# Low parts of every second first-layer weight tile subtracted by GpSimd instead of VectorE

## The chip, the cores and the metric

The kernel runs on one core of a Trainium2 chip. The metric is the device time of one execution in microseconds, the median of several runs. The engines of a core work side by side, each through its own queue in order: TensorE (PE; its weight loads are shown as PEld), VectorE (DVE), ScalarE (ACT), GpSimd (POOL) and SyncE (SP), which issues all the DMAs here.

## What is computed

A windowed attention with 32 global tokens (4 batches, 8 heads, 512 local tokens each), and behind it two feed-forward layers over 2304 tokens, 512 wide with 2048 hidden units. The weights come in as 64-bit floats.

```python
def _moe_ref(x, w_in, w_out):          # first layer
    h = x @ w_in
    relu6 = np.clip(h + 3.0, 0.0, 6.0)
    g = h * relu6 / 6.0
    return (g @ w_out).astype(np.float32)

def _moe2_ref(x, w_in, w_out):         # second layer
    h = x @ w_in
    g = np.where(h > 0.0, h, np.exp(np.minimum(h, 0.0)) - 1.0)
    return (g @ w_out).astype(np.float32)
```

## The kernel before

Every product of the feed-forward layers is made from split operands: a number is kept as a high part, rounded to the format of the fast matrix product (fp32r), and a low part, which is the number minus its high part; three products (high by high, high by low, low by high) replace one. The first layer's weights are split into 16 tiles, one for each 128 hidden units. A tile `f` holds 128 x 512 numbers of `w_in` and 128 x 512 of `w_out`, so 1024 columns, and it is prepared in four steps by the class `Split`:

- `first` (line 126, ScalarE): converts the upper halves of the 64-bit words to a float in the buffer `f`.
- `second` (line 130, VectorE): a shift of that buffer.
- `third` (lines 134 and 137, VectorE): two merges of bits, each reading the raw words and the buffer, both in SBUF, and writing the buffer. The second needs the first's result.
- `fourth` (line 147, ScalarE, and 148, VectorE): the cast to the high part, then buffer minus high part, which gives the low part. Both operands of this subtraction lie in SBUF.

The buffer `f` has three places that the tiles use in turn (`f % 3`), so `first` of tile `k` waits until the subtraction of tile `k - 3` has read its buffer. Tile 0 is prepared in two halves, the others whole.

All this happens during the first 130 us, in between other work: the attention of the first tokens, and the first token chunk's passes through the layer. For a hidden tile `f` the pass is `up` (12 products on TensorE into `h`; the third one is the first that needs the low part of the weights), `act` (an activation of `h` on ScalarE, L600; a min-and-multiply on VectorE, L601, which reads `g` in SBUF and `h` in PSUM; a cast on ScalarE, L606; and a subtraction on VectorE, L608, which reads `g` and `gh` in SBUF and makes `gl`), and `down` (12 products into `acc`, the second of which needs `gl`). The attention's row minimum on VectorE (L390) reads one operand in PSUM and one in SBUF.

The order of all of it up to 130 us is written out by hand in a string, `SCHED`, read from left to right, and each step issues its instructions at that point. A letter is a step and a number its tile: `a`, `b`, `c`, `d` are the four steps of `Split`, `U` is `up`, `R` the activation and L601 and L606, `L` is L608, `D` is `down`; other letters load or belong to the attention. So the queue of every engine follows this string. After it a loop runs the other token chunks, and the second layer's weights are prepared beside them (`prepare`), starting with two loads (L160) into the buffers `f0` and `f2`, the first of which waits for the last subtraction of tile 15.

GpSimd has little to do: it makes the identity matrix at the start and, after 420 us, two subtractions of 128x768 (L668).

Of the kernel before, what the change touches and what calls it, by code (L numbers as in the profile page):

```python
# [10 lines left out]
F32 = mybir.dt.float32  # L11
# [57 lines left out]
def tile_kernel(ctx, tc, qkW, vW, qkG, vN, vG, masks, w1, w2, out):  # L69
    nc = tc.nc  # L70
# [41 lines left out]
    class Split:  # L112
# [28 lines left out]
        def fourth(self, s=slice(2)):  # L141
            if s.start in (None, 0):
                wslot[self.m, self.f] = pool.tile(
                    [P, 2, 2, DM], F32R, name=f"w{self.m}_{self.f}", tag="w", bufs=NF
                )
            hi, lo = wslot[self.m, self.f][:, 0], wslot[self.m, self.f][:, 1]
            nc.scalar.copy(hi[:, s], self.wf[:, s])
            nc.vector.tensor_sub(lo[:, s], self.wf[:, s], hi[:, s].bitcast(F32))  # L148

    splits = [Split(0, f) for f in range(NF)]  # L150
    wd = [dr.tile([P, 12 * DM], F32, name=f"wd{p}", tag=f"wd{p}") for p in range(NF // 2)]
# [183 lines left out]
    class Local:  # L335
# [111 lines left out]
        def stages(self, nxt=None):  # L447
            def first():
                self.scores()
                for r in range(2):  # L450
                    self.softmax(r)
                if nxt is not None:
                    nxt.load_qk()

            def second():
                for r in range(2):
                    self.transposed(r)

            def third():
                self.values()  # L460
                self.normalised()
                if nxt is not None:
                    nxt.load_v()

            def fourth():
                self.turned()
                self.split()

            loads = ((1.9, 1.8), (0, 1.2), (1.2, 0), (0.7, 0.6))
            if self.n < CHUNKS[0] + CHUNKS[1]:  # L470
                loads = ((1.9, 1.8), (0, 1.2), (0.4, 1.8), (0.7, 0.6))
            return list(zip((first, second, third, fourth), loads))
# [198 lines left out]
    class Super:  # L671
# [139 lines left out]
        def up(self, g, k):  # L811
# [11 lines left out]
            if k == 1:  # L823
                self.s1 = self.staged(g, "s1", "gh")
                nc.scalar.copy(self.s1, self.a)
            elif k == 2:
                self.c11 = self.staged(g, "c11", "gl")
                nc.vector.tensor_add(self.c11, self.b, self.s1)  # L828
                self.after(1, lambda c=self.c11: self.act(g, 0, c))
            elif k == 6:  # L830
                self.s2 = self.staged(g, "s2", "gh")
                nc.scalar.copy(self.s2, self.a)
            elif k == 5:
                s4, c22 = self.staged(g, "s4", "gh"), self.staged(g, "c22", "gl")
                nc.scalar.copy(s4, self.a)  # L835

                def fourth(b=self.b):
                    nc.vector.tensor_add(c22, b, s4)
                    self.after(1, lambda: self.act(g, 3, c22))

                self.after(1, fourth)
            elif k == 3:
                self.act(g, 1, self.a)
            elif k == 4:
                c21 = self.staged(g, "c21", "gl")
                nc.vector.tensor_add(c21, self.b, self.s2)
                self.after(2, lambda: self.act(g, 2, c21))
# [243 lines left out]
```

## Time and profile before

| | |
|---|---|
| median of 3 runs | 864.99 us (864.95 to 866.28) |
| the profiled execution, its own time | 864.55 us |
| its span, first to last instruction | 862.8 us |
| TensorE busy | 841.0 us, 97% |
| VectorE busy | 516.3 us, 60% |
| ScalarE busy | 429.5 us, 50% |
| GpSimd busy | 4.4 us, 1%, 8 instructions |
| mean granted TensorE clock | 0.997 |

Busy time is the sum of the instructions' durations on an engine; it is an average over stages that differ. The stage of the first 130 us is read apart in the rows below. A start of an instruction is given in us from the span's beginning; its row may name in brackets how long the engine sat idle before it, and what ended that.

### The profile page before, as it was taken

How to read it: one execution, taken by the hardware profiler on the slowest of the kernel's cores; microseconds unless marked ns; L12 is line 12 of the kernel's file. 1: busy time of each engine (PE TensorE's matmuls, PEld its weight loads, DVE VectorE, ACT ScalarE, POOL GpSimd, SP SyncE). 2: the span in 40 equal slices, each digit the busy share in tenths (PEclk: the TensorE clock that was granted, in tenths of full speed). 3: DMA queues.
4: the chain of work that ended last, by engine and by line, in shares of the span. 5: the costliest groups of instructions: out<-in, count | busy, mean ns of one | idle time of the engine just before them, and what ended most of it. 6: DMA issues, size and time to landing. Idle time of an engine off the chain costs nothing.

```text
span 862.8 us, 15804 instructions
## 1 busy us (share of the span) xinstructions
PE 841.0 (97%) x6424; PEld 727.1 (84%) x6424; DVE 516.3 (60%) x1125; ACT 429.5 (50%) x835; POOL 4.4 (1%) x8
## 2 busy tenths in 40 slices
PE   8899999999999999998999999999999999999997
PEld 7677778898988899887888889998998888888886
DVE  5788984666565556664655557444456665445443
ACT  6577655454544455543433346454445664444441
POOL 0000000000000000000000000000000000000000
PEclk9999999999999999999999999999999999999999
DMA  9958213656674765563589783946852656444102
GB/s 370 418 210 327 84 52 108 229 180 196 235 258 136 236 230 201 196 201 117 190 296 330 271 315 142 385 172 265 344 187 84 258 208 255 147 147 147 49 1 98
DMA packets 37657, 178.43 MB, mean 207 GB/s; under 512 B 4304, under 2 KB 6224, under 8 KB 25680
## 3 DMA queue, kind: packets, MB, share of 16 engines
q1 hardware_dynamic: 37584, 177.42, 56.9%
q8 instruction: 50, 0.82, 0.4%
q14 instruction: 23, 0.19, 0.1%
HBM read 143.33 MB, written 34.08 MB: 206 GB/s over the span
## 4 chain that ended last, share of the span: by engine, by line
PE 84%; DVE 7%; DMA 4%; ACT 3%; issue 2%; SPq 0%; ACTq 0%; DVEq 0%
PE acc L574 30%; PE h L574 22%; PE ua L574 9%; PE yt L574 9%; PE ub L574 7%; DMA v<-in_vW 1%; PE O L413 1%; PE S L381 1%; PE T L90 1%; DVE f L134 1%; DVE g L601 1%; DVE f L137 1%; DMA raw<-in_w 1%; DVE w L148 1%; DMA qk<-in_qkW 1%
## 5 line engine op out<-in xcount | busy, mean ns | idle before, releaser
L574 PE MATMUL acc<-gh,w 128*128 128x384 f32 (+1 forms) x640 | 199.5, 367 | 0.0
L574 PE MATMUL h<-x1h,w 128*128 128x384 f32 (+1 forms) x640 | 195.7, 367 | 1.6 <-DVE w L148 1.5
L574 PEld LDWEIGHTS h<-x1h,w 128*128 128x128 f32 x640 | 118.5, 189 | 20.1 <-issue 5.3
L574 PEld LDWEIGHTS acc<-gh,w 128*128 128x128 f32 x640 | 119.1, 189 | 13.4 <-issue 0.6
L574 PE MATMUL acc<-gl,w 128*128 128x384 f32 (+1 forms) x320 | 115.6, 361 | 0.8 <-DVE gl L608 0.8
L574 PE MATMUL h<-x1l,w 128*128 128x384 f32 (+1 forms) x320 | 115.5, 361 | 0.2 <-DVE x1l L445 0.2
L601 DVE SCALAR_TENSOR_TENSOR g<-g,h 128x384 f32<-128x384 f32 (+1 forms) x80 | 48.6, 607 | 110.4 <-ACT g L600 110.2
L600 ACT ACTIVATE g<-h,half 128x384 f32<-128x384 f32 (+1 forms) x80 | 49.8, 622 | 93.0 <-PE h L574 92.9
L606 ACT CAST gh<-g 128x384 fp32r<-128x384 f32 (+1 forms) x96 | 52.8, 550 | 77.0 <-DVE g L601 64.9
L574 PE MATMUL ua<-xs,ws 128*128 128x384 f32 (+1 forms) x384 | 88.0, 364 | 0.0
L574 PEld LDWEIGHTS ua<-xs,ws 128*128 128x128 f32 x384 | 70.4, 188 | 10.7 <-ACT s L835 0.3
L608 DVE TENSOR_TENSOR gl<-g,gh 128x384 fp32r<-128x384 f32 (+1 forms) x96 | 57.4, 599 | 24.6 <-ACT gh L606 24.1
L574 PEld LDWEIGHTS acc<-gl,w 128*128 128x128 f32 x320 | 60.4, 189 | 6.5 <-DVE gl L608 1.2
L574 PE MATMUL ub<-xs,ws 128*128 128x384 f32 (+1 forms) x288 | 65.7, 363 | 0.0
L574 PEld LDWEIGHTS h<-x1l,w 128*128 128x128 f32 x320 | 60.4, 189 | 6.1 <-DVE x1l L445 0.5
L574 PEld LDWEIGHTS ub<-xs,ws 128*128 128x128 f32 x288 | 52.7, 188 | 7.0
L877 DVE TENSOR_TENSOR y<-yt,y 128x512 f32<-128x512 f32 x49 | 33.8, 690 | 36.0 <-PE yt L574 35.5
L792 ACT ACTIVATE e<-c 128x384 f32<-128x384 f32 (+1 forms) x48 | 27.8, 580 | 45.8 <-DVE c L828 15.8
L574 PE MATMUL acc<-ws,gg_h 128*128 128x512 f32 x160 | 49.9, 393 | 0.0
L574 PE MATMUL yt<-ws,gg_h 128*128 128x512 f32 x160 | 49.9, 393 | 0.0
L795 DVE SCALAR_TENSOR_TENSOR e<-e,c 128x384 f32<-128x384 f32 (+1 forms) x48 | 30.0, 624 | 23.9 <-ACT e L793 23.3
L793 ACT ACTIVATE e<-e 128x384 f32<-128x384 f32 (+1 forms) x64 | 37.1, 579 | 2.0
(202 smaller groups left out, 1260.2 us busy)
## 6 DMA issues: line engine op xcount, KB each, us to landing
ws<-wd SPq DMA_DIRECT2D x48, 1024.0 KB, 5.4
raw<-in_w SPq DMA_DIRECT2D x16, 1024.0 KB, 11.7
raw<-in_w SPq DMA_DIRECT2D x32, 512.0 KB, 5.4
v<-in_vW SPq DMA_DIRECT2D x13, 1040.0 KB, 6.6
qk<-in_qkW SPq DMA_DIRECT2D x15, 704.0 KB, 6.0
qkG<-in_qkG SPq DMA_DIRECT2D x8, 608.0 KB, 4.6
wd<-ha SPq DMA_DIRECT2D x8, 512.0 KB, 4.8
wd<-hb SPq DMA_DIRECT2D x8, 512.0 KB, 4.8
```

What stands on the lines that cost most here:

```text
L90: nc.tensor.transpose(o, i, ident)
L134: nc.vector.scalar_tensor_tensor(w, self.high[:, s], -0x80000000, w, op0=ALU.bitwise_and, op1=ALU.bitwise_or)
L137: nc.vector.scalar_tensor_tensor(w, self.low[:, s], 29, w, op0=ALU.logical_shift_right, op1=ALU.bitwise_or)
L574: nc.tensor.matmul(o, a, b, start=first and i == 0, stop=last and i == len(pairs) - 1, skip_group_check=more)
L600: nc.scalar.activation(g, hp, AF.Relu, scale=1.0 / 6.0, bias=half)
L601: nc.vector.scalar_tensor_tensor(g, g, 1.0, hp, op0=ALU.min, op1=ALU.mult)
L606: nc.scalar.copy(gh, g)
L608: return lambda: nc.vector.tensor_sub(gl, g, gh.bitcast(F32))
L792: nc.scalar.activation(e, h, AF.Relu, scale=-1.0)
L793: nc.scalar.activation(e, e, AF.Exp, scale=-1.0)
L795: 1, lambda: nc.vector.scalar_tensor_tensor(e, e, -1.0, h, op0=ALU.add, op1=ALU.max)
L877: nc.vector.tensor_add(y, o, y)
```

## The change

The subtraction of `Split.fourth` is issued on GpSimd for tiles with an odd number (1, 3, ... 15) and stays on VectorE for even ones.

```diff
             hi, lo = wslot[self.m, self.f][:, 0], wslot[self.m, self.f][:, 1]
             nc.scalar.copy(hi[:, s], self.wf[:, s])
-            nc.vector.tensor_sub(lo[:, s], self.wf[:, s], hi[:, s].bitcast(F32))
+            sub = nc.gpsimd.tensor_sub if self.f % 2 else nc.vector.tensor_sub
+            sub(lo[:, s], self.wf[:, s], hi[:, s].bitcast(F32))
```

The line it adds shifts the numbers of all later lines by one, so L148 is L149 after, L601 is L602, and so on. Two places of the program show what it does to the queues. The first is VectorE's queue around tiles 5 and 6, before and then after; `f0_6` is the buffer of tile 6, `w0_5` the finished tile 5, `g0_0_3` the activation of hidden tile 3, and the brackets name the counters that an instruction waits for.

```order
L601 SCALAR_TENSOR_TENSOR g0_0_3_909<-g0_0_3_909,h0_0_3_840 128x512 [waits Activation_49]
L130 TENSOR_SCALAR f0_6_889<-f0_6_889 128x1024
L134 SCALAR_TENSOR_TENSOR f0_6_889<-raw0_6_697,f0_6_889 128x1024 [waits DMAHW4_49,DVE_49]
L137 SCALAR_TENSOR_TENSOR f0_6_889<-raw0_6_697,f0_6_889 128x1024 [waits DVE_49]
L148 TENSOR_TENSOR w0_5_931<-f0_5_836,w0_5_931 128x1024 [waits Activation_49]
L148 TENSOR_TENSOR w0_6_934<-f0_6_889,w0_6_934 128x1024 [waits Activation_49]
L608 TENSOR_TENSOR gl0_0_3_911<-g0_0_3_909,gh0_0_3_910 128x512
```

After it, the same stretch of VectorE's queue:

```order
L602 SCALAR_TENSOR_TENSOR g0_0_3_909<-g0_0_3_909,h0_0_3_840 128x512 [waits Activation_49]
L130 TENSOR_SCALAR f0_6_889<-f0_6_889 128x1024 [waits Pool_49]
L134 SCALAR_TENSOR_TENSOR f0_6_889<-raw0_6_697,f0_6_889 128x1024 [waits DMAHW4_49,DVE_49]
L137 SCALAR_TENSOR_TENSOR f0_6_889<-raw0_6_697,f0_6_889 128x1024 [waits DVE_49]
L149 TENSOR_TENSOR w0_6_934<-f0_6_889,w0_6_934 128x1024 [waits Activation_49]
L609 TENSOR_TENSOR gl0_0_3_911<-g0_0_3_909,gh0_0_3_910 128x512
```

The subtraction of tile 5 is gone from between the second merge of tile 6 and the subtraction of tile 6; nothing else changes place.

The second place is ScalarE's queue around tiles 7 to 9, before and then after; `f0_10` is the conversion (`first`) of tile 10 into the buffer that tile 7 used.

```order
L147 CAST w0_7_1160<-f0_7_891 128x1024
L126 ACTIVATE f0_10_1170<-raw0_10_1044 128x1024 [waits DMAHW4_49,DVE_49]
L147 CAST w0_8_1189<-f0_8_993 128x1024
L147 CAST w0_9_1192<-f0_9_1046 128x1024 [waits DMAHW5_49,DVE_49]
L600 ACTIVATE g0_0_7_1196<-h0_0_7_1176,half_65 128x512 [waits PE_49]
```

After it, the same stretch of ScalarE's queue:

```order
L147 CAST w0_7_1160<-f0_7_891 128x1024
L126 ACTIVATE f0_10_1170<-raw0_10_1044 128x1024 [waits DMAHW4_49,Pool_49]
L147 CAST w0_8_1189<-f0_8_993 128x1024
L147 CAST w0_9_1192<-f0_9_1046 128x1024 [waits DMAHW5_49,DVE_49]
L601 ACTIVATE g0_0_7_1196<-h0_0_7_1176,half_65 128x512 [waits PE_49]
```

The order is the same; the conversion of tile 10 now waits for GpSimd where it waited for VectorE, and the casts of tiles 8 and 9 still stand behind it. On GpSimd's queue the eight subtractions follow each other in the order of the tiles, each waiting for ScalarE's cast of its tile, ahead of the two of L668.

## Rows read from the trace of the kernel before

**Rows 1.** Windows: stretch, busy us and instructions by engine, clock, DMA share, GB/s.
```profile
35.00:60.00 25.00, 24.69 (x230) 18.89 (x229) 22.15 (x42) 19.54 (x36) 0.00 (x0) 1.00 0.79 318
60.00:90.00 30.00, 27.71 (x239) 20.93 (x238) 27.39 (x50) 18.63 (x37) 0.00 (x0) 1.00 0.58 236
90.00:130.00 40.00, 40.00 (x297) 31.95 (x296) 35.27 (x56) 23.88 (x43) 0.00 (x0) 1.00 0.22 76
```

**Rows 2.** Chain that ended last, two pieces: start, us, engine, output, line.
```profile
63.88 1.23 DVE f L137
...
87.01 2.60 PE h L574 x10
```

**Rows 3.** Waits of TensorE, 28 to 130 us: waiter, releaser, us, times, longest.
```profile
PE h L574 <- DVE w L148: 1.5, 2, 1.2
```

**Rows 4.** Groups by shape: operation, count, busy us and mean ns, idle before.
```profile
L668 POOL TENSOR_TENSOR x2l<-x2raw,x2h 128x768 fp32r<-128x768 f32 x2 | 3.7, 1845 | 436.5 <-ACT x2h L667 436.5
...
L148 DVE TENSOR_TENSOR w<-f,w 128x1024 fp32r<-128x1024 f32 x15 | 18.3, 1221 | 5.7 <-ACT w L147 5.7
...
L183 DVE TENSOR_TENSOR ob<-wo,ob 128x512 fp32r<-128x512 f32 x8 | 5.5, 689 | 1.6 <-ACT ob L179 1.6
```

**Rows 5.** Timeline, GpSimd and VectorE about 440 us: start, us, engine, operation, idle before.
```profile
439.64 1.85 POOL L668 TENSOR_TENSOR x2l<-x2raw,x2h 128x768 fp32r<-128x768 f32 x1 [14.86 <-ACT x2h L667]
...
440.11 1.92 DVE L183 TENSOR_TENSOR oa<-wo,oa 128x512 fp32r<-128x512 f32 x1 [0.56 <-ACT oa L179]
```

**Rows 6.** Timeline of VectorE about tiles 1 to 4.
```profile
36.63 1.22 DVE L148 TENSOR_TENSOR w<-f,w 128x1024 fp32r<-128x1024 f32 x1
37.76 1.22 DVE L134 SCALAR_TENSOR_TENSOR f<-raw,f 128x1024 int32<-128x1024 int32 x1
...
47.79 1.22 DVE L148 TENSOR_TENSOR w<-f,w 128x1024 fp32r<-128x1024 f32 x1
...
49.54 1.29 DVE L134 SCALAR_TENSOR_TENSOR f<-raw,f 128x1024 int32<-128x1024 int32 x1
```

**Rows 7.** Timelines of VectorE and of ScalarE about tiles 5 and 6.
```profile
65.03 2.41 DVE L148 TENSOR_TENSOR w<-f,w 128x1024 fp32r<-128x1024 f32 x2
67.36 0.69 DVE L608 TENSOR_TENSOR gl<-g,gh 128x512 fp32r<-128x512 f32 x1
...
62.54 1.05 ACT L147 CAST w<-f 128x1024 fp32r<-128x1024 f32 x1
65.14 1.05 ACT L147 CAST w<-f 128x1024 fp32r<-128x1024 f32 x1 [1.55 <-DVE f L137]
```

**Rows 8.** Timelines of VectorE and of ScalarE about tiles 7 to 10.
```profile
81.47 1.23 DVE L148 TENSOR_TENSOR w<-f,w 128x1024 fp32r<-128x1024 f32 x1 [2.33 <-ACT w L147]
...
84.59 1.23 DVE L137 SCALAR_TENSOR_TENSOR f<-raw,f 128x1024 int32<-128x1024 int32 x1
...
82.73 1.16 ACT L126 ACTIVATE f<-raw 128x1024 f32<-128x1024 f32 x1 [1.29 <-DVE w L148]
83.79 1.04 ACT L147 CAST w<-f 128x1024 fp32r<-128x1024 f32 x1
```

**Rows 9.** Timeline of TensorE: products that need `gl` (68.97) or a weight's low part.
```profile
68.97 0.39 PE L574 MATMUL acc<-gl,w 128*128 128x512 f32 x1
...
82.75 0.73 PE L574 MATMUL h<-x1h,w 128*128 128x512 f32 x2
...
87.01 0.73 PE L574 MATMUL h<-x1h,w 128*128 128x512 f32 x2 [1.19 <-DVE w L148]
```

**Rows 10.** TensorE's longest wait near 400 us, and the window (as rows 1) behind it.
```profile
399.87 0.84 PE L90 MATMUL XTG<-ident,xgg 128*128 128x128 f32 x4 [2.59 <-DVE xgg L554]
...
400.00:404.00 4.00, 4.00 (x16) 4.00 (x16) 1.84 (x5) 1.04 (x4) 0.00 (x0) 0.57 0.40 127
```

**Rows 11.** Second layer's first weight loads on SyncE's queue, and ScalarE's first use.
```profile
128.07 0.80 SPq L160 DMA_DIRECT2D raw<-in_w  x2
...
143.50 0.68 ACT L164 ACTIVATE wi<-raw 128x512 f32<-128x512 f32 x1
```

## The prediction

> **What bounds the kernel now.** I read the busy time by stretch first, then who waits for whom on TensorE, then the chain that ended last, then the queues around the eight moved subtractions. The busy shares say that TensorE is the bound of the whole: between 90 and 130 us it is busy 40.00 of 40 us [rows 1], and after that it waits only in a few places that the change doesn't touch. Whatever TensorE loses while the first layer's weights are being prepared is therefore lost at the end too, and whatever it gains there is gained. Between 35 and 90 us it is busy 24.69 of 25 and 27.71 of 30, so it idles 2.6 us there, and VectorE is almost as full: 22.15 of 25 and 27.39 of 30 [rows 1]. In that stretch the chain runs through VectorE: its second bit-merge (L137) at 63.88 is on it, and the chain returns to TensorE at 87.01 for good [rows 2]. TensorE's own waits on the moved line amount to 1.5 us in two places [rows 3]. So this is a stage with two full engines; a microsecond more on VectorE shows at the end, a microsecond less is worth 2.6 us altogether at most.
>
> **What the change takes away and adds.** Eight subtractions of 128x1024 (tiles 1, 3, ... 15) leave VectorE. One takes 1.22 us, and the next one starts 1.14 us after it, since ends overlap [rows 4, 6]. Half of them stand between 35 and 90 us: 4 x 1.14 = 4.6 us of VectorE's queue. GpSimd is idle there, and it has done the same operation in this trace, on 768 columns in 1.845 us [rows 4]. By columns, 1024 take 1.845 x 1024/768 = 2.46 us; if it scales as VectorE's does with part of it fixed, some 2.36. I take 2.46. No instruction or DMA is added, and TensorE's order is the same.
>
> **The price that decides: VectorE stands still meanwhile.** The trace has one place where VectorE's subtraction of two SBUF tiles met GpSimd's. GpSimd ran from 439.64 for 1.85 us, to 441.49. VectorE's 128x512 subtraction was begun at 440.11 and took 1.92 us, to 442.03 [rows 5], where the same one takes 0.69 us otherwise [rows 4]. It ended 0.54 us after GpSimd did, so it made no progress until GpSimd was through and then needed all but 0.15 us of its normal time. GpSimd took 1.85 us with and without that neighbour (the mean of the two is 1.845). I carry this over: a VectorE operation that reads two SBUF tiles (the merges L134 and L137, the subtractions L148 and L608) stops until GpSimd's subtraction ends, and a 128x1024 one ends 1.22 - 0.15 = 1.07 us after it. The trace doesn't show what happens to an operation with one operand in PSUM (L601, L390), or which of the two is let in when both are ready; I take the first as free and the second as whoever comes first. The Trainium skill (SBUF — State Buffer, Who interferes with whom) says the same: a VectorE instruction with two SBUF inputs contends with a GpSimd instruction that reads SBUF, and the one that starts first holds the shared ports for the whole instruction while the other is fully blocked. The trace agrees, with the 1.92 us for 0.69.
>
> So each moved subtraction gives VectorE 1.14 us and can take up to 2.46. Walking down the queues:
>
> **Tile 1.** GpSimd can take it where VectorE did, at 36.63 to 36.7, and ends it at 39.15. VectorE's next operation, the first merge of tile 2 (37.76 before), would now start at once, is stopped, and ends at 39.15 + 1.07 = 40.2 instead of 37.76 + 1.22 = 39.0 [rows 6]. VectorE is 1.2 us late.
>
> **Tile 3.** From 47.79 + 1.2 = 49.0 to 51.5 on GpSimd. VectorE does one free operation (L601) beside it; the first merge of tile 4 (49.54 for 1.29 us before, so to 50.83) is stopped and ends at 51.5 + 1.07 = 52.55 [rows 6]. VectorE is 1.75 us late.
>
> **Tile 5.** Its cast on ScalarE ends at 62.54 + 1.05 + 1.75 = 65.35 [rows 7]. The second merge of tile 6 depends on the first and would start at 63.88 + 1.75 = 65.63 [rows 2]; in that joint GpSimd gets in, from 65.6 to 68.05, and the merge ends at 69.1. Only then can ScalarE cast tile 6 (released by that merge, 1.05 us), which before was hidden by VectorE's subtraction of tile 5: the two subtractions ran back to back in 2.41 us. Now VectorE waits for the cast until 70.2 and subtracts to 71.35, where L608 follows, which stood at 67.36 [rows 7]. VectorE is 4.0 us late: the 1.14 us taken from it here are lost again as a wait for ScalarE. If the merge gets in first, it is 2.95. TensorE needs what L608 makes at 68.97 [rows 9]; it was there at 67.36 + 0.69 = 68.05, so of the 4.0 us, 3.1 reach TensorE.
>
> **Tile 7.** VectorE waited 2.33 us for this tile's cast and subtracted at 81.47; now the cast is ready at 85.5. VectorE, without the wait and the subtraction, is by then in the second merge of tile 9 (84.59 + 4.0 - 2.33 - 1.14 = 85.1, to 86.25) [rows 8]; behind it GpSimd runs to 88.7. Two things hang on that. TensorE's third product of this tile, at 82.75 before [rows 9], starts at 88.75, 6.0 us late, after 6.0 - 3.1 = 2.9 us of idling. And ScalarE's conversion of tile 10, which takes over tile 7's buffer and waited for the subtraction before as well (82.73), holds the cast of tile 8 behind it (83.79) [rows 8]: both are 6.0 us late, the cast ends at 90.85, VectorE's subtraction of tile 8 at 92.0, and TensorE's product that waited for it at 87.01 [rows 9] could start at 92.05, 5.05 us late.
>
> **The clock.** TensorE has idled as long once in this trace: before 399.87 for 2.59 us, and then the granted clock was 0.57 on average over 400 to 404 us, that is mostly the lower of its two levels (1.2 of 2.4 GHz) [rows 10]: 4 x 0.43 = 1.7 us lost. After the 2.9 us at tile 7 I expect that once more. From the product of 82.75 to the wait that ended at 87.01 TensorE had 4.26 - 1.19 = 3.1 us of work; it comes there at 88.75 + 3.1 + 1.7 = 93.5, later than tile 8's 92.05, and is 6.5 us late.
>
> **Tiles 9 to 15.** Behind tile 8 VectorE has 40 - 35.27 = 4.7 us to spare before 130 us [rows 1]. Three tiles (9, 11, 13) give back 3.4 us and stop it for at most 7.4, a net 4.0, so its lead over TensorE shrinks but lasts, and I put them at nothing; with that lead gone they would cost up to 1.3 us each. Tile 15 frees the buffer into which SyncE loads the second layer's first weights: they left at 128.07, and leave some 8 us later. They are first used at 143.50 [rows 11], which is itself 6 to 7 us later, so it costs nothing.
>
> **Sum.** 6.5 us, all of it by tile 8. The profiled execution took 864.55 us (its span 862.8 and 1.75 around it), 0.44 us under the median 864.99: 864.55 + 6.5 = 871.05, and by the median **871.5 us**. With the merge first at tile 5, 2.36 us for one subtraction and no fall of the clock it is some 4 us (869); with the unlucky order at every tile some 8 to 9 us (873.5).
>
> **Rivals.** One: the two engines don't stop each other. For it speaks that only one meeting is on record; against it, that this meeting is plain. VectorE would then run ahead where it is on the chain, but only by 0.4 us, because ScalarE's casts and activations come next. At tile 7 the subtraction itself, 2.46 for 1.22 us, lies between the cast and TensorE and, through tile 10's conversion, ahead of tile 8's cast: 0.8 us late at 82.75, made up by the 1.19 us wait that TensorE had at 87.01. Gain and loss cancel: **865.0 us**, not slower. It decides if the merges keep their 1.22 us beside GpSimd.
> Two: VectorE stops whatever it does, L601 and L390 with a PSUM operand too. Then all eight tiles cost 2.46 - 1.14 = 1.32 us, or 10.6 us, and the free operations of tiles 3 and 11 give no cover: **875.6 us**. For it: nothing in the trace tells those operations apart; against it, between tiles 9 and 15 the spare 4.7 us absorb part.
> Three: most meetings fall into VectorE's idle time, and only tile 7's longer way (about 2 us) shows: **867 us**. Against it stands how full VectorE is.
>
> **Chances and range.** The forecast 0.74, rival one 0.10, two 0.10, three 0.06. Something like 0.2% (1.7 us) is what a measurement of this kernel can tell from no change; rival one lies within it, with 0.02 for a small gain. So slower 0.89, same 0.09, faster 0.02. The range runs from 867.0 (rival three) to 876.0 (rival two) and leaves out rival one and little else.
>
> **What would show it.** In the profile after: GpSimd rows of 128x1024 at about 2.4 us, eight of them; L134, L137 or L608 with single durations near 2 to 3.5 us where GpSimd ran; a wait of TensorE for GpSimd at tile 7 of 2 to 3 us, with a granted clock near 0.5 behind it; a wait of VectorE for ScalarE's cast of tile 6. It is wrong if the merges keep 1.22 us throughout, if GpSimd needs under 1.5 us, or if TensorE's idle time between 35 and 90 us is not some 6 us above the 2.6 of before.

## The result, and the profile after

The changed kernel takes **869.74 us** (median of 5 runs, 868.49 to 871.46); the kernel before, run beside it, 864.99 us (864.39 to 866.28). The ratio is 1.0053, with a 95% interval of 1.0037 to 1.007: **4.75 us slower, 3.2 to 6.0**. That lies in the forecast range (867.0 to 876.0) and 1.8 us under the forecast of 871.5. The profiled execution took 868.84 us, its span 866.7 us.

The busy times of the whole page answer first what the change did to VectorE. GpSimd rose from 4.4 to 25.5 us, and VectorE did not fall: 516.3 us before, now 516.2.

```profile
PE 844.6 (97%) x6424; PEld 729.2 (84%) x6424; DVE 516.2 (60%) x1117; ACT 429.1 (50%) x835; POOL 25.5 (3%) x16
```

Eight subtractions of 1.22 us, 9.8 us of VectorE, were taken away. The groups by shape (operation, count, busy us and mean ns, idle before) show where they came back. The first row is GpSimd's, the others VectorE's.

```profile
L149 POOL TENSOR_TENSOR w<-f,w 128x1024 fp32r<-128x1024 f32 x8 | 21.1, 2640 | 113.0 <-ACT w L147 113.0
...
L609 DVE TENSOR_TENSOR gl<-g,gh 128x512 fp32r<-128x512 f32 x32 | 25.3, 792 | 8.0 <-ACT gh L607 7.6
L134 DVE SCALAR_TENSOR_TENSOR f<-raw,f 128x1024 int32<-128x1024 int32 x15 | 21.0, 1402 | 0.2
L137 DVE SCALAR_TENSOR_TENSOR f<-raw,f 128x1024 int32<-128x1024 int32 x15 | 20.7, 1379 | 0.5
L149 DVE TENSOR_TENSOR w<-f,w 128x1024 fp32r<-128x1024 f32 x7 | 9.5, 1362 | 9.3 <-ACT w L147 9.3
```

In the kernel before, the same groups are:

```profile
L608 DVE TENSOR_TENSOR gl<-g,gh 128x512 fp32r<-128x512 f32 x32 | 21.9, 686 | 8.1 <-ACT gh L606 7.6
L134 DVE SCALAR_TENSOR_TENSOR f<-raw,f 128x1024 int32<-128x1024 int32 x15 | 18.5, 1231 | 0.2
L137 DVE SCALAR_TENSOR_TENSOR f<-raw,f 128x1024 int32<-128x1024 int32 x15 | 18.5, 1231 | 0.5
```

Nothing in these operations changed, yet they grew by 3.4, 2.5 and 2.2 us, and the seven subtractions left on VectorE by 7 x 0.14 = 1.0 us against their 1221 ns of before [rows 4]. That is 9.1 of the 9.8 us. A mean hides what happened: the timeline (start, us, engine, line, operation, idle before and what ended it) shows a few single instructions that took 1.4 to 4 times their length. GpSimd's subtractions of tiles 1, 3, 5, 7 and 9:

```profile
36.39 2.59 POOL L149 TENSOR_TENSOR w<-f,w 128x1024 fp32r<-128x1024 f32 x1 [35.09 <-ACT w L147]
48.52 2.75 POOL L149 TENSOR_TENSOR w<-f,w 128x1024 fp32r<-128x1024 f32 x1 [9.54 <-ACT w L147]
65.24 2.41 POOL L149 TENSOR_TENSOR w<-f,w 128x1024 fp32r<-128x1024 f32 x1 [13.97 <-ACT w L147]
85.21 3.00 POOL L149 TENSOR_TENSOR w<-f,w 128x1024 fp32r<-128x1024 f32 x1 [17.56 <-ACT w L147]
91.34 2.52 POOL L149 TENSOR_TENSOR w<-f,w 128x1024 fp32r<-128x1024 f32 x1 [3.12 <-ACT w L147]
```

VectorE at the same times, and the wait that followed at tile 6 and at tile 8:

```profile
36.72 3.37 DVE L134 SCALAR_TENSOR_TENSOR f<-raw,f 128x1024 int32<-128x1024 int32 x1
...
50.02 0.69 DVE L602 SCALAR_TENSOR_TENSOR g<-g,h 128x512 f32<-128x512 f32 x1 [1.04 <-ACT g L601]
50.62 1.78 DVE L134 SCALAR_TENSOR_TENSOR f<-raw,f 128x1024 int32<-128x1024 int32 x1
...
65.45 3.28 DVE L137 SCALAR_TENSOR_TENSOR f<-raw,f 128x1024 int32<-128x1024 int32 x1
69.84 1.23 DVE L149 TENSOR_TENSOR w<-f,w 128x1024 fp32r<-128x1024 f32 x1 [1.12 <-ACT w L147]
70.99 0.68 DVE L609 TENSOR_TENSOR gl<-g,gh 128x512 fp32r<-128x512 f32 x1
...
90.35 1.22 DVE L149 TENSOR_TENSOR w<-f,w 128x1024 fp32r<-128x1024 f32 x1 [4.40 <-ACT w L147]
91.49 2.92 DVE L609 TENSOR_TENSOR gl<-g,gh 128x512 fp32r<-128x512 f32 x1
```

Add start and length. GpSimd at tile 1 ends at 38.98, and the merge beside it at 40.09, 1.11 us later. At tile 3 the ends are 51.27 and 52.40 (1.13), at tile 5 67.65 and 68.73 (1.08). At tile 9, 93.86 and 94.41 (0.55, a half-size operation). So a stopped operation does nearly all its work after GpSimd's end, as in the one meeting of before [rows 5]. L602 at 50.02, with one operand in PSUM, kept its 0.69 us in the middle of GpSimd's run.

TensorE's waits from 28 to 140 us (waiter, releaser, us in total, times, longest), the answer to [rows 3]:

```profile
PE acc L575 <- DVE gl L609: 2.7, 3, 1.2
PE h L575 <- POOL w L149: 2.1, 1, 2.1
```

Before, the second of these did not exist, and the first was:

```profile
PE acc L574 <- DVE gl L608: 0.8, 1, 0.8
```

What did exist before was 1.5 us for VectorE's low part [rows 3], of which 0.2 is left. The windows (stretch, busy us and count for PE, PEld, DVE, ACT, POOL, then clock, DMA share, GB/s) answer [rows 1], with four single microseconds behind tile 7 among them:

```profile
35.00:60.00 25.00, 23.67 (x224) 17.47 (x223) 21.09 (x39) 17.88 (x34) 5.34 (x2) 1.00 0.80 322
60.00:90.00 30.00, 25.52 (x224) 18.79 (x223) 24.56 (x43) 17.61 (x35) 5.42 (x2) 0.97 0.59 235
88.00:89.00 1.00, 0.73 (x2) 0.64 (x3) 0.00 (x0) 0.75 (x1) 0.21 (x1) 0.74 0.00 0
89.00:90.00 1.00, 1.00 (x4) 0.71 (x4) 0.00 (x0) 1.00 (x2) 0.00 (x0) 0.50 0.00 0
90.00:91.00 1.00, 1.00 (x4) 0.81 (x3) 0.65 (x1) 1.00 (x2) 0.00 (x0) 0.50 0.00 0
91.00:92.00 1.00, 1.00 (x4) 0.78 (x3) 1.00 (x2) 0.26 (x1) 0.66 (x1) 0.56 0.00 0
90.00:130.00 40.00, 40.00 (x293) 31.84 (x292) 37.14 (x55) 24.84 (x44) 7.93 (x3) 0.98 0.20 72
```

TensorE idles 1.33 + 4.48 = 5.8 us between 35 and 90 us, where it was 2.6, and after the gap at tile 7 it runs at the lower clock level: 0.26 + 0.5 + 0.5 + 0.44 = 1.7 us lost by these windows. By the products it is a little less: the nine from the third of tile 7 on took 3.75 us (88.27 to 92.02), 2.20 before (82.75 to 84.95), so 1.55 us lost. The same three products on TensorE as in [rows 9]:

```profile
71.73 0.50 PE L575 MATMUL acc<-gl,w 128*128 128x512 f32 x1 [1.20 <-DVE gl L609]
...
88.27 1.06 PE L575 MATMUL h<-x1h,w 128*128 128x512 f32 x2 [2.09 <-POOL w L149]
...
92.72 0.63 PE L575 MATMUL h<-x1h,w 128*128 128x512 f32 x2
```

The last row is the third product of tile 8; it stood at 87.01 before.

To measure the stage by itself I use two marks that every kernel has: the first product of `up` with real data and the first scores of a later attention block, `S`. Before:

```profile
35.47 0.48 PE L574 MATMUL h<-x1h,w 128*128 128x512 f32 x1
...
96.98 1.16 PE L381 MATMUL S<-qk 64*32 64x128 f32 x64
```

After:

```profile
35.43 0.48 PE L575 MATMUL h<-x1h,w 128*128 128x512 f32 x1
...
102.59 1.16 PE L382 MATMUL S<-qk 64*32 64x128 f32 x64
```

**The stage** takes 61.51 us before and 67.16 us after: 5.65 us longer. From `S` to the transposes of line 90 near 400 us the two executions differ by 0.5 us the other way (302.89 and 302.39), and from there to the end by 1.2 us (462.93 and 461.72). The 1.2 us lie behind TensorE's last products, before and then after:

```profile
852.09 5.72 PE L574 MATMUL acc<-ws,gg 128*128 128x512 f32 x24
...
857.20 5.72 PE L575 MATMUL acc<-ws,gg 128*128 128x512 f32 x24
```

They come 5.1 us later, as the transposes near 400 us do, but the span ends 5.0 us behind them before and 3.8 us after. So the stage lost more than the spans show (862.8 and 866.7), and the interval of the medians, 3.2 to 6.0, holds both.

### The profile page after: what moved, and what is told of

It reads as the page before. It is cut to its first block, busy times and chain, and to the rows that moved or that the text cites. A ratio compares the mean times of both kernels' runs of the same rounds, so it can differ in the third digit from the quotient of the medians.

```text
span 866.7 us, 15814 instructions
## 1 busy us (share of the span) xinstructions
PE 844.6 (97%) x6424; PEld 729.2 (84%) x6424; DVE 516.2 (60%) x1117; ACT 429.1 (50%) x835; POOL 25.5 (3%) x16
## 4 chain that ended last, share of the span: by engine, by line
PE 87%; DVE 4%; issue 3%; ACT 3%; DMA 2%; POOL 0%; SPq 0%; ACTq 0%; DVEq 0%; POOLq 0%
PE acc L575 31%; PE h L575 24%; PE ua L575 9%; PE yt L575 9%; PE ub L575 7%; PE O L414 2%; PE S L382 2%; PE T L90 1%; DMA qk<-in_qkW 1%; DVE f L134 1%; PE SG L504 1%; PE OG L532 1%; DVE g L602 1%; ACT g L601 1%; DVE x1l L446 1%
## 5 line engine op out<-in xcount | busy, mean ns | idle before, releaser
L602 DVE SCALAR_TENSOR_TENSOR g<-g,h 128x384 f32<-128x384 f32 (+1 forms) x80 | 48.5, 606 | 114.0 <-ACT g L601 114.0
L601 ACT ACTIVATE g<-h,half 128x384 f32<-128x384 f32 (+1 forms) x80 | 49.8, 623 | 95.1 <-PE h L575 94.8
L609 DVE TENSOR_TENSOR gl<-g,gh 128x384 fp32r<-128x384 f32 (+1 forms) x96 | 60.8, 634 | 24.5 <-ACT gh L607 24.1
```

The source lines that it names most:

```text
L601: nc.scalar.activation(g, hp, AF.Relu, scale=1.0 / 6.0, bias=half)
L602: nc.vector.scalar_tensor_tensor(g, g, 1.0, hp, op0=ALU.min, op1=ALU.mult)
L609: return lambda: nc.vector.tensor_sub(gl, g, gh.bitcast(F32))
```

## The experiments

Theory: GpSimd's subtraction and VectorE's operations on two SBUF tiles stop each other, that delays VectorE's chain at tiles 1, 3 and 5, GpSimd's longer way opens a gap at tile 7, the clock falls behind the gap, and tiles 9 to 15 cost nothing. Rivals: the loss is all the longer way of one subtraction at tile 7; VectorE stops whatever it does; the late tiles cost too. Each edit is shown against the changed kernel where nothing else is said, "the stage" is the time between the two marks, and the kernel before was run beside each. A stage is read from one traced execution of each kernel. Two kernels were traced twice, and their stages agreed within 0.2 us (60.23 and 60.30, 60.39 and 60.22).

### Only tile 7 on GpSimd

```diff
-            sub = nc.gpsimd.tensor_sub if self.f % 2 else nc.vector.tensor_sub
+            sub = nc.gpsimd.tensor_sub if self.f in (7,) else nc.vector.tensor_sub
```

> Only tile 7's subtraction is on GpSimd, all others on VectorE. Theory of stops (VectorE's loss by being stopped at tiles 1, 3 and 5 makes the first part of the time lost): here nothing of VectorE meets GpSimd's run, so only the longer way from cast to low part counts. Tile 7's third product at 84.7 us instead of 82.75, tile 8's at 88.1 instead of 87.01; +1.1 us in all if the clock stays, about +2.5 if it falls behind the 2 us of idling. Rival, the longer way at tile 7 is everything: +4.75, as with all eight.

Measured: 864.8 us, ratio 0.9998 (0.9988 to 1.0007). This execution had a fall of the clock ahead of the stage, so it is measured from the first product `O` behind tile 3 to `S`: 20.28 us before (76.70 to 96.98), 21.20 here (78.42 to 99.62), so 0.92 us lost; by the two marks (37.26 to 99.62) it is 0.85. TensorE had the gap at tile 7, 1.89 us, and the product that waited 1.19 us for tile 8 before waits 0.29 us now.

```profile
86.30 0.73 PE L575 MATMUL h<-x1h,w 128*128 128x512 f32 x2 [1.89 <-POOL w L149]
...
89.66 0.73 PE L575 MATMUL h<-x1h,w 128*128 128x512 f32 x2 [0.29 <-DVE w L149]
```

The granted clock stayed at 1.00 behind that gap. So a gap of 1.9 us is made by the longer way alone, and half of it is made up one tile later by a wait that was there anyway. The longer way is not the whole loss. The medians don't confirm the 0.92 us: their interval reaches up to 0.6, and the trace is one execution.

### Only tiles 1, 3 and 5 on GpSimd

```diff
-            sub = nc.gpsimd.tensor_sub if self.f % 2 else nc.vector.tensor_sub
+            sub = nc.gpsimd.tensor_sub if self.f in (1, 3, 5) else nc.vector.tensor_sub
```

> Tiles 1, 3 and 5 are on GpSimd, all others on VectorE. Theory of stops: the merges of tiles 2, 4 and 6 last 3.4, 1.8 and 3.3 us as with all eight, TensorE's product that needs gl is at 71.7 us instead of 68.97, and because tile 7 follows on a late VectorE, the low part of tile 8 comes 3.6 us late: +2.8 to +3.6 us in all, no fall of the clock. Rival, the longer way at tile 7 is everything: 0 to +0.5.

Measured: 867.22 us, ratio 1.0034 (1.0021 to 1.0047), so 2.9 us slower by the ratio, 2.4 by the medians; the stage took 65.16 us (35.12 to 100.28), 3.65 us more than before, without a fall of the clock. TensorE's waits (28 to 140 us):

```profile
PE acc L575 <- DVE gl L609: 2.7, 3, 1.2
PE h L575 <- DVE w L149: 1.7, 3, 1.2
```

The first row is word for word that of the changed kernel. In this kernel no product waits for GpSimd at all; TensorE waits for VectorE, whose queue was made shorter. These three tiles are the largest part of the loss.

### Only tiles 9 to 15 on GpSimd

```diff
-            sub = nc.gpsimd.tensor_sub if self.f % 2 else nc.vector.tensor_sub
+            sub = nc.gpsimd.tensor_sub if self.f in (9, 11, 13, 15) else nc.vector.tensor_sub
```

> Tiles 9, 11, 13 and 15 are on GpSimd, all others on VectorE. Theory of stops with slack: VectorE is stopped there too (single durations of 1.9 to 2.9 us), but TensorE is ahead of nothing and waits for nothing: within 0.5 us of before. Rival, every stop costs wherever it is: 4 x 1.3 = +5 us.

Measured: 863.59 us, ratio 0.9991 (0.9979 to 1.0003); the stage took 61.49 us (35.22 to 96.71), 0.02 us less. The stops are there, they only cost nothing. On VectorE:

```profile
87.85 2.27 DVE L130 TENSOR_SCALAR f<-f 128x1024 int32<-128x1024 int32 x1
...
102.11 1.87 DVE L609 TENSOR_TENSOR gl<-g,gh 128x512 fp32r<-128x512 f32 x1
```

The first row is new: L130, a shift with a single operand, takes 0.68 us otherwise and was stopped to 0.55 us behind GpSimd's end (86.71 + 2.86 = 89.57).

The three parts give 0.92 + 3.65 - 0.02 = 4.55 us; all eight together lose 5.65. What the parts don't have is the fall of the clock.

### The clock, with TensorE kept busy at tile 7

Fourteen products of the identity matrix with itself are issued ahead of tile 7's `up` (a step `z14` in the order).

```diff
-... D5.1 b9 a10 c9 W14 U7 d8 d9 ...
+... D5.1 b9 a10 c9 W14 z14 U7 d8 d9 ...
```

> The changed kernel with 14 products of the identity by itself put on TensorE ahead of tile 7's first product (about 1.8 us of work into a bank that the first product then overwrites). Theory that the granted clock's fall behind the 2.1 us of idling makes about 1 us of the loss: the idle time at tile 7 shrinks under 0.5 us, the clock stays at its upper level, tile 7's third product stays at 88.3 us, and TensorE is 4.6 us late at the row of scores that stood at 96.98 us, instead of 5.6: +3.6 us in all instead of +4.75. Rival, the clock's fall is covered by the wait for tile 8: still 5.6 us late.

Measured: 871.7 us, ratio 1.0078 (1.0064 to 1.0092), above the change itself, though the two were not run side by side and the intervals of their ratios overlap. The stage took 66.29 us (35.42 to 101.71): 0.87 us less than the changed kernel's, at a clock of 1.00 throughout. But I had sized the filling wrongly: the trace has two products for each that the program writes, 28 for 3.29 us, and the product behind them started 0.4 us after GpSimd's subtraction had ended. And behind `S` this execution lost 305.44 - 302.39 = 3.05 us against the changed kernel's: 0.5 us in a wait for tile 13's low part on GpSimd, 1.4 us more in the waits for `x1l` (4.0 for 2.6), and the rest about a fall of the clock between 240 and 260 us (0.91 on average), where the changed kernel's was 1.00. Why these last two grew stays open. The same with eight:

```diff
-... D5.1 b9 a10 c9 W14 U7 d8 d9 ...
+... D5.1 b9 a10 c9 W14 z8 U7 d8 d9 ...
```

> The changed kernel with 8 identity products issued ahead of tile 7's product; with 14 of them the trace had 28 products that took 3.29 us and ended 0.4 us after GpSimd's subtraction, so they filled the gap but pushed tile 7's third product 0.8 us further. Eight should take about 1.9 us and end before the subtraction does. From the first h product to the scores row S6: the changed kernel lost 5.65 us, the three parts alone 4.55. Theory (the part above 4.55 is the fall of TensorE's clock after tile 7's idle): granted clock 1.00 at 88 to 92 us, third product of tile 7 at 88.1 to 88.4 us, loss 4.3 to 4.8 us, and about 0.9 to 1.3 us less than the changed kernel in the median if nothing else differs later. Rival (the part above 4.55 is VectorE's lateness at tile 8, whatever the clock): loss stays 5.4 to 5.9 us although the clock stays.

Measured: 869.64 us, ratio 1.0055 (1.0041 to 1.0068); the stage took 66.04 us (35.99 to 102.03), **4.53 us** more than before, against 4.55 for the three parts (an agreement closer than two traces of one kernel have). Clock and tile 7's gap in this kernel:

```profile
89.00:90.00 1.00, 1.00 (x6) 0.78 (x6) 0.00 (x0) 1.00 (x2) 0.00 (x0) 1.00 0.07 16
90.00:91.00 1.00, 1.00 (x6) 0.82 (x5) 0.21 (x1) 1.00 (x2) 0.00 (x0) 1.00 0.00 0
```

```profile
86.03 1.95 PE L99 MATMUL h<-ident 128*128 128x128 f32 x16
...
88.71 0.73 PE L575 MATMUL h<-x1h,w 128*128 128x512 f32 x2 [0.26 <-POOL w L149]
...
92.06 0.73 PE L575 MATMUL h<-x1h,w 128*128 128x512 f32 x2 [0.30 <-DVE w L149]
...
124.97 0.73 PE L575 MATMUL h<-x1h,w 128*128 128x512 f32 x2 [0.79 <-POOL w L149]
```

The filling did not delay the product that matters (88.71 - 35.99 = 52.72 us behind the first mark; 88.27 - 35.43 = 52.84 in the changed kernel), and the stage became 1.12 us shorter. That is the price of the fall of the clock in the traced execution of the changed kernel. It is less than the 1.55 us that the products lost, because without the fall TensorE reaches tile 8's low part too early and waits 0.30 us for VectorE (the row at 92.06). The median did not follow (the two kernels were not run side by side). In the trace, 0.56 us were lost ahead of the first mark, where this execution's clock fell (0.91 on average from 20 to 40 us), and the last row says where 0.8 us more went: TensorE, earlier than in the changed kernel, now meets tile 13's low part, which GpSimd finishes no earlier (it starts it 85.93 us behind the first mark in both kernels; with the late tiles alone on GpSimd it was 80.59). In the changed kernel this wait doesn't exist. So the late tiles cost nothing as long as TensorE is as late as the engines that prepare them, or those engines are not late either.

### What stops VectorE: a fill, and a copy, in place of the subtraction

In both kernels GpSimd writes the low part of the odd tiles without computing it, so those eight subtractions are left out. The edits are against the kernel before. First a fill, which reads nothing:

```diff
-            nc.vector.tensor_sub(lo[:, s], self.wf[:, s], hi[:, s].bitcast(F32))
+            if self.f % 2:
+                nc.gpsimd.memset(lo[:, s].bitcast(F32), 0.0)
+            else:
+                nc.vector.tensor_sub(lo[:, s], self.wf[:, s], hi[:, s].bitcast(F32))
```

> GpSimd only fills the low parts of the odd tiles with zeros, so those subtractions are left out of the computation; VectorE's queue is that of the changed kernel. It tells whether VectorE is stopped by GpSimd's reading, or by its running at all. Theory of stops by reading: a fill reads nothing, the merges keep 1.22 us, VectorE is 1.14 us ahead at each odd tile, and TensorE's waits of before on VectorE vanish in part: -0.5 to -2.2 us. Rival, any GpSimd instruction on SBUF stops VectorE: merges longer by up to the fill's duration, no gain.

Measured: 861.61 us, ratio 0.9967 (0.995 to 0.9984); the stage took 59.24 us (35.91 to 95.15), 2.27 us less than before. VectorE beside a fill:

```profile
89.76 0.96 POOL L149 MEMSET w<- 128x1024 f32 x1 [10.93 <-DVE f L137]
...
90.07 0.68 DVE L611 TENSOR_TENSOR gl<-g,gh 128x512 fp32r<-128x512 f32 x1
```

A subtraction of two SBUF tiles in the middle of GpSimd's fill keeps its 0.68 us. Then a copy, which reads one tile:

```diff
-            nc.vector.tensor_sub(lo[:, s], self.wf[:, s], hi[:, s].bitcast(F32))
+            if self.f % 2:
+                nc.gpsimd.tensor_copy(lo[:, s], self.wf[:, s])
+            else:
+                nc.vector.tensor_sub(lo[:, s], self.wf[:, s], hi[:, s].bitcast(F32))
```

> GpSimd copies the buffer into the low parts of the odd tiles, so that it reads one tile and writes one; those subtractions are left out of the computation. It tells whether reading one tile is enough to stop VectorE. Theory, any reading by GpSimd stops VectorE's operations on two SBUF tiles: merges and subtractions are stopped until the copy ends, for as long as the copy takes (1 to 1.5 us), and the time lies between that with the fill (-3) and that with the subtraction (+4.75), about 0. Rival, only a GpSimd operation that reads two tiles does: merges keep 1.22 us and the time is as with the fill, less what the waits for the cast cost, -2 us.

Measured: 862.57 us, ratio 0.9976 (0.9962 to 0.999); the stage took 60.05 us (35.71 to 95.76), 1.46 us less than before. VectorE beside the copy:

```profile
96.64 1.04 POOL L149 CAST w<-f 128x1024 fp32r<-128x1024 f32 x1 [12.44 <-DVE f L137]
...
96.93 1.29 DVE L611 TENSOR_TENSOR gl<-g,gh 128x512 fp32r<-128x512 f32 x1
```

The same operation takes 1.29 us and ends 0.54 us after GpSimd's 97.68. So it is GpSimd's reading that stops such an operation, and one tile read is enough. The time alone would not have told: it came out 2.2 us below the kernel before, near the rival's -2 and not at the theory's 0, since only four of the eight copies met an operation that they stop, and the four rows grew by 2.2 us in all. The rows decide. The Trainium skill (SBUF — State Buffer, Who interferes with whom) draws the same line, a GpSimd instruction that reads against one that only writes, and the two rows agree with it. The fill also bounds the idea behind the change: VectorE's relief without any stop, and without a wait for ScalarE's cast, which the fill doesn't need, is worth 2.3 us of the stage.

### Two pairs of steps exchanged

The kernel before, all subtractions on VectorE, with two merges issued ahead of a subtraction and a shift ahead of another.

```diff
-... W9 D1.0 d4 c5 a6 a7 ...
+... W9 D1.0 c5 d4 a6 a7 ...
-... D5.0 d7 D5.1 b9 a10 ...
+... D5.0 b9 d7 D5.1 a10 ...
```

> The kernel before, all subtractions on VectorE, with two steps exchanged in the order: tile 5's merges ahead of tile 4's subtraction and tile 9's shift ahead of tile 7's, so that VectorE works where it waited 2.33 us for ScalarE's casts. Theory that VectorE is the bound of 35 to 90 us and its waits are what can be won: VectorE is 2 us ahead behind tile 5, TensorE's waits of 0.76 and 1.19 us vanish or shrink: -1 to -2 us. Rival, ScalarE's casts bound it as well: 0 to -0.5.

Measured: 863.88 us, ratio 0.9991 (0.9979 to 1.0004); the stage took 60.23 us (34.95 to 95.18), 1.28 us less. The waits of TensorE for `gl` are gone, and 0.7 us are left of the 1.5 for VectorE's low part. Then the same order with tiles 9 to 15 on GpSimd, the only ones that cost nothing:

```diff
-            sub = nc.gpsimd.tensor_sub if self.f % 2 else nc.vector.tensor_sub
+            sub = nc.gpsimd.tensor_sub if self.f % 2 and self.f >= 9 else nc.vector.tensor_sub
```

> Only tiles 9 to 15 subtract on GpSimd, and two pairs of steps of the order are exchanged (c5 before d4, b9 before d7), which with all subtractions on VectorE gained 1.28 us in the stretch to the scores row S6; the GpSimd part alone gave -0.02 us there. Theory (the two are independent, since the exchanged steps are at tiles 4 to 9 and GpSimd's first subtraction comes behind them): stretch 1.0 to 1.5 us shorter than before's 61.51, total 863 to 864.3. Rival (the stops at tiles 9 and 11 fall on a VectorE that has less slack in the new order): the gain is lost, stretch within 0.4 us of before.

Measured: 862.35 us, ratio 0.9964 (0.995 to 0.9977); the stage took 60.39 us (35.17 to 95.56), 1.12 us less. This is faster than both kernels, but it was not run beside the order alone. So these two kernels once more, side by side on one chip:

> The two exchanged pairs of the order (c5 before d4, b9 before d7) with all subtractions on VectorE, on one chip with the next kernel, which differs from it only by GpSimd's subtractions of tiles 9 to 15. In the stretch to the scores row S6 the traces so far give -1.28 us for this one and -1.12 us with GpSimd; the medians -0.9 and -2.8 us were taken apart. Theory (the order alone makes the gain): both the same within 1 us, 863 to 864. Rival (GpSimd's late tiles are worth a further 1.5 to 2 us behind the scores row): this one 1.5 to 2 us above the next.

> The exchanged order with tiles 9 to 15 on GpSimd, beside the kernel that has the order alone. Theory: 863 to 864, within 1 us of it, and a stretch to the scores row about 1.1 us shorter than before's. Rival: 1.5 to 2 us below it.

Measured: 862.80 us for the order alone (0.9977, 0.9967 to 0.9987) and 862.84 us with GpSimd's late tiles (0.9982, 0.9972 to 0.9992); stages of 60.30 and 60.22 us. The rival falls: the order makes the gain, some 1.6 to 2 us, and GpSimd adds nothing to it. Part of what this kernel lacked, then, was the right thing at the head of VectorE's queue (1.2 to 1.3 us of the stage). Relief would be worth something too, if it came without stops: the fill had 2.3 us.

## Why the prediction was right, point by point

**The price that decides** was carried over from one meeting, and it held. A stopped operation ends 1.08 to 1.13 us after GpSimd where 1.07 was put, and the fill and the copy show that it is the reading that does it. Rival one (no stop) falls with the merges of 3.37 and 3.28 us. Rival two (everything stops) falls with L602 at 50.02, 0.69 us beside GpSimd, and with the row minimum L391, which kept its 0.27 us beside tile 11's subtraction. Rival three (only tile 7's longer way shows) falls with the parts: tiles 1, 3 and 5 lose 3.65 us of the stage, tile 7 alone 0.92. The list of operations that stop was one short: L130, with one operand, stops too (2.27 for 0.68 us). It mattered little here: at tiles 1 and 3 it was ahead of GpSimd, which waited for it and took 2.59 and 2.75 us.

**GpSimd's subtraction** was put at 2.46 us by columns, with 2.36 as the other end; undisturbed it takes 2.41 and 2.44 (tiles 11 and 15). Where VectorE was in the middle of an operation first, GpSimd's own row is longer (3.00 at tile 7, where the merge L137 ran from 84.73 for 1.23 us). The forecast let it run behind that merge too.

**Tiles 1 and 3.** The stopped merges were to end at 40.2 and 52.55; they end at 40.09 and 52.40.

**Tile 5.** GpSimd did get into the joint between the two merges, at 65.24 (65.6 was forecast), the merge ended at 68.73 (69.1), VectorE waited 1.12 us for ScalarE's cast of tile 6, and `gl`'s subtraction started at 70.99 (71.35), 3.63 us late instead of 4.0. TensorE got it at 71.73, 2.76 us late where 3.1 was put.

**Tile 7.** The third product came at 88.27, for 88.75. The idle time was 2.09 us, not 2.9: the product came 0.5 us earlier than forecast, and TensorE itself reached that point later, through small waits that the sum left out (one of 0.33 us at 79.95 for ScalarE).

**The clock** fell as forecast, and the lower level took 1.7 us by the windows, as put, or 1.55 by the products. Its net price is 1.12 us, measured by the kernel that kept TensorE busy; most of the rest lies over a wait for tile 8 that stands there otherwise. That it fell was in part luck. The gap was 2.09 us, shorter than the 2.59 us from which the forecast was carried over, and the wait near 400 us shows that not even that one always brings a fall: in all thirteen traces TensorE waits there for 2.58 to 2.60 us, in twelve the clock then goes to 0.50, and in one, of the exchanged order alone, it stays. These are the products that waited, and a window as in [rows 1], its clock third from the end:

```profile
398.01 0.63 PE L90 MATMUL XTG<-ident,xgg 128*128 128x128 f32 x4 [2.58 <-DVE xgg L554]
...
398.00:404.00 6.00, 5.99 (x35) 5.97 (x36) 2.73 (x7) 2.49 (x7) 0.00 (x0) 1.00 0.49 167
```

The same kernel, traced another time, had 0.72 over the same 6 us. So how many executions of the changed kernel pay the 1.12 us is not known.

**Tile 8.** VectorE's low part was done at 91.57 (forecast 92.0), and the product that needs it stands in the trace at 92.72 (93.5). Before it was 87.01, so 5.7 us late instead of 6.5. This is the term that was too large, by 0.8 us: 0.5 us of it came with tile 7, and the way from there to tile 8 took 4.45 us where 4.75 was put.

**Tiles 9 to 15** cost nothing, alone (-0.02 us) as in the changed kernel. Behind that lies a condition that the prediction named as a lead over TensorE: in the kernel with eight identity products TensorE came to tile 13 1.12 us earlier, counted from the first mark, and waited 0.79 us there. The loads behind tile 15 left 7.4 us late (135.44 for 128.07), and ScalarE used them 5.6 us late, at 149.12. One count was wrong: tile 9's subtraction stood back to back with tile 8's at 85.73, so five of the eight lay between 35 and 90 us, not half of them. No later term of the sum uses it.

**The sum** was 6.5 us, the stage lost 5.65, the medians 4.75. The last 0.9 us are not explained by the stage. In the two profiled executions the changed one gains 0.5 us between `S` and 400 us, nothing from there to TensorE's last product (the fall of the clock near 400 us is in both), and 1.2 us behind it. That end behind the last product was 3.7 to 3.9 us in every traced kernel with three or more tiles on GpSimd, and 4.1 to 5.0 us in the others. Why it is shorter stays open, and the prediction had no term for it.

**The signs** came as named, but for one. TensorE's idle time between 35 and 90 us was to be some 6 us above the 2.6 of before, or the prediction was wrong; it is 3.2 above. The sign does not follow from the prediction's own sum: its waits of 3.1 and 2.9 us, less the 1.19 us that vanish at 87.01, are 4.8 us of idle time, and the other 1.7 of the 6.5 are the clock, in which TensorE is busy. Of the 4.8, 0.8 are the shorter gap at tile 7. The stage's 5.65 us are 3.20 of idle time and 2.45 of busy time, of which the clock is 1.55; the remaining 0.9 stand in rows that the profile counts as busy, as 1.1 us do in the kernel with tiles 1, 3 and 5 alone. Which rows, I have not worked out.

## What to carry to other kernels

Before moving work from VectorE to GpSimd, look for one place in the trace where the two already meet: if VectorE's operation ends a fixed time after GpSimd's, the move takes VectorE's time rather than giving it, here 9.1 of 9.8 us. A queue that is the bound at a few points may want its steps in another order, not fewer of them: two exchanged pairs gained what eight moved subtractions could not. And a loss has to be measured part by part, since the parts (4.55 us) missed what showed only with all of them together (1.1 us of clock in the traced execution).

## What the runs showed of the hardware that was not expected

- The stop goes both ways. GpSimd's subtraction, 2.41 to 2.44 us with nothing in its way, took 2.59, 2.75 and 3.00 us where VectorE was in the middle of L130 or L137 at its start; each time it ended 2.25 to 2.30 us after VectorE's operation did.
- A one-operand shift stops as well: L130, 0.68 us for 1024 columns where the two-operand merges need 1.23, took 2.27 us beside GpSimd's subtraction and 1.53 us beside its copy. The Trainium skill (SBUF — State Buffer, Who interferes with whom) names such an operation if it runs in one of VectorE's two-port modes; the short time fits that, but no run here tells the mode.
- Gaps of nearly the same length had different ends: behind 1.89 us of idling at tile 7, in the kernel with that tile only, the granted clock stayed at 1.00; behind 2.09 us in the changed kernel it went to 0.50. The changed kernel had also idled more ahead of it, 1.6 us from 65.9 to 85.9 against 0.3 in the 20 us ahead of the other gap. Which of the two differences did it, or whether either had to, the runs don't say, since the wait near 400 us, 2.58 to 2.60 us in every trace, once brought no fall at all.
